# Batch 0's scatter places cast one by one on GpSimd, and block plans cut to the blocks they have

## The chip, the cores and the metric

The kernel runs on one core of one Trainium2 chip. The metric is device microseconds of one execution. The kernel before was timed three times: 1270.5, 1272.84 and 1274.08 us, median 1272.84 us.

A core has a matrix engine (TensorE, PE in the profile; PEld is its loading of stationary operands), a vector engine (VectorE, DVE), a scalar engine (ScalarE, ACT), GpSimd (POOL) and SyncE (SP), which here only issues DMAs. Each engine works through its own instructions in order and waits on semaphores for the others.

## The reference

Two blocks follow each other: an FNet mixing (the real part of a two-dimensional Fourier transform over sequence and feature) and a mixture of experts without dropped tokens, in which each token goes to the one expert with the largest logit.

```python
x: (8, 2496, 256)                                  # batch, sequence, feature
X = np.fft.fft(np.fft.fft(x, axis=1), axis=2).real
x = X.reshape(8 * 2496, 256)                       # 19968 tokens
logits = x @ w_gate                                # w_gate (256, 8)
expert_idx = np.argmax(logits, axis=1)
probs = softmax(logits)                            # 1e-9 added to the sum
for e in range(8):                                 # tokens sorted by expert
    h = np.maximum(x_sorted[lo:hi] @ w1[e], 0.0)   # w1 (8, 256, 1024)
    y_sorted[lo:hi] = h @ w2[e]                    # w2 (8, 1024, 256)
return gate_w[:, None] * y                         # in the tokens' own order
```

## The kernel before

The eight batches of the input go through four stages, and later batches' early stages are woven into earlier batches' late ones.

1. `first(b)`: SP loads the batch in three thirds (tile `xq`, line 289), VectorE folds it (`fold`, lines 295 to 306: wide additions and subtractions of two operands), TensorE makes the first Fourier step, and the result goes to DRAM (`Td`, line 342) and back in another layout (`regroup`, line 354).
2. `second(b)`: the further Fourier steps, in two halves of ten tiles of 128 rows. For each tile ScalarE and VectorE write the transformed rows to the tile `rows` (lines 384 and 410) and the logits to `lg` (408).
3. `route(b, h, rows, lg)`: once per half. VectorE finds each token's expert; TensorE counts ranks (`rk`); VectorE sums up the place of each token in the sorted buffer `Xs` in DRAM (lines 450 to 455). The places come out as a 128 x 10 tile, one column for each of the ten tiles, and the ten scatters are put on the list `waiting`.
4. `send()` takes one scatter from that list: an indirect DMA on GpSimd's queue (`put_row`, line 236), which writes 128 rows of 258 floats to the places in an int32 column `pi`. For batches 1 to 7 the place is float: ScalarE copies the column to a small tile `due` (line 468) and GpSimd casts it to `pi` (line 469). For batch 0 VectorE writes the int32 tile `pi` in the last addition of the places (line 453), and the scatter follows without a cast.

When both halves of a batch are routed, `close(b)` runs `plan(b, size, k, last)` for each block size of that batch's round: which rows of `Xs`, of which expert, each of the `k` blocks takes. This is a string of about 20 small VectorE operations on one partition (lines 488 to 521), and it leaves a table `tab`. The round of batch 0 has a plan of 2 blocks of 256 tokens and one of 4 blocks of 128; then follow 4 of 256, 3 of 512, and 5 of 512 for each of the batches 3 to 7; the last round also has 7 of 256 and 21 of 128. `MOST` is the largest of these counts, 21, and the plan's larger tiles are all made for 21 entries.

`experts(todo)` then works through the blocks. SP reads an entry of the table into registers and loads the block's weights (`fetch_weights`, lines 544 and 546) and its rows from `Xs` (`fetch_rows`, four DMAs from line 534 and one from line 538). The read of rows waits until all scatters of the batches in that round have landed; the loading of weights only needs the table. VectorE transposes the rows (line 582), TensorE makes the two products with a ReLU between them (lines 796 and 798), and the scaled rows go out by indirect DMA from GpSimd.

The order is fixed when the program is built. Batch 0 goes first: `send()` is called once after each step of `second(0)`, so that the first half's scatters are issued while the second half is being transformed; what is left of them is issued before the first block. After that, steps of batch b + 1 are put between the blocks of batch b - 1's and b's rounds by a counter of due steps.

Of the kernel before, what the change touches and what calls it, by code (L numbers as in the profile page):

```python
# [15 lines left out]
ALU = mybir.AluOpType  # L16
ACTF = mybir.ActivationFunctionType
AX_X = mybir.AxisListType.X
# [17 lines left out]
E, F = 8, 1024  # L36
# [14 lines left out]
def bc(ap, axis, n):  # L51
    shape = list(ap.shape)
    shape.insert(axis, n)
    return ap[tuple([slice(None)] * axis + [None])].to_broadcast(shape)
# [75 lines left out]
def rounds():  # L130

    want = [((256, 2), (128, 4)), ((256, 4),)] + [((512, B),)] * (B - 2)
    plan, used = [], 0

    def full(done, size):
        return max(0, -(-(done - used - E * (size - 1)) // size))

    for b in range(B):  # L140
        done = (b + 1) * S
        now = []
        for size, most in want[b]:
            k = min(full(done, size), most)
            if k:
                now.append((size, k, False))
            used += size * k
        if b == B - 1:
            k = full(done, BLK)
            used += BLK * k  # L150
            now.append((BLK, k, False))
            now.append((REST, (NT - used + E * (REST - 1)) // REST, True))
        plan.append(now)
    return plan
# [33 lines left out]
MOST = max(k for now in rounds() for _, k, _ in now)  # L188
# [27 lines left out]
def kernel(ctx: ExitStack, tc, x, w_gate, w1, w2, out):  # L216
    nc = tc.nc
    vec, act, pool = nc.vector, nc.scalar, nc.gpsimd

    def mm(o, lhsT, rhs, start=True, stop=True, **kw):  # L220
        nc.tensor.matmul(o, lhsT=lhsT, rhs=rhs, start=start, stop=stop, **kw)  # L221
# [13 lines left out]
    def put_row(dst, idx, rows, last, group):  # L235
        return unordered(pool.indirect_dma_start(  # L236
            out=dst, out_offset=bass.IndirectOffsetOnAxis(ap=idx, axis=0),
            in_=rows, in_offset=None, bounds_check=last, oob_is_err=False), group)


    def sent(ins, b):
        tc.declare_no_dep(ins, group="taken", reason="no block before this batch's round has these rows")
        tc.add_to_no_dep_group(f"xs{b}", ins)
# [25 lines left out]
    con, k = {}, 0  # L269
# [146 lines left out]
    def route(b, h, rows, lg):  # L416

        nonlocal base

        def small(name, *dims, dt=F32):  # L420
            return sp.tile([128, *dims], dt, tag=name, name=name)

        mx, eq, v = small("mx", NSL), small("eq", NSL, E), small("v", NSL)
        vec.reduce_max(mx[:], lg[:], axis=AX_X)
        vec.tensor_tensor(eq[:], lg[:], bc(mx[:], 2, E), op=ALU.is_equal)
        vec.tensor_tensor(eq[:], eq[:], bc(con["rev"][:], 1, NSL), op=ALU.mult)
        vec.reduce_max(v[:], eq[:], axis=AX_X)
        vec.tensor_tensor(v[:], v[:], con["good"][:, h], op=ALU.mult)
        oh = small("oh", NSL + 1, E, dt=BF16)
        vec.memset(oh[:, NSL], 0.0)  # L430
        vec.tensor_tensor(oh[:, 0:NSL], bc(con["rev"][:], 1, NSL), bc(v[:], 2, E), op=ALU.is_equal)
        yield

        su = small("su", NSL)
        vec.tensor_tensor(lg[:], lg[:], bc(mx[:], 2, E), op=ALU.subtract)
        act.activation(lg[:], lg[:], ACTF.Exp)
        vec.tensor_scalar(rows[:, :, D], con["row"][:, h], float(b * S), None, op0=ALU.add)
        yield

        rk = pm_.tile([128, NSL + 1, E], F32, tag="m", name="rk")  # L440
        mm(rk[:], tri[:], oh[:], True, False)
        for s in range(NSL):
            mm(rk[:, s + 1:], ones[:], bc(oh[:, s], 1, NSL - s), False, s == NSL - 1)
        vec.reduce_sum(su[:], lg[:], axis=AX_X)
        vec.tensor_scalar(su[:], su[:], 1e-9, None, op0=ALU.add)
        vec.reciprocal(rows[:, :, D + 1], su[:])
        yield

        pos, pf, pi = small("pos", NSL, E), small("pf", NSL), small("pi", NSL, dt=I32)
        vec.tensor_tensor(pos[:], rk[:, 0:NSL], bc(base[:], 1, NSL), op=ALU.add)  # L450
        vec.tensor_tensor(pos[:], pos[:], oh[:, 0:NSL], op=ALU.mult)
        vec.reduce_sum(pf[:], pos[:], axis=AX_X)
        vec.tensor_tensor(pf[:] if b else pi[:], pf[:], con["far"][:, h], op=ALU.add)
        nxt = cp.tile([128, E], F32, tag="base", name="base", bufs=2)
        vec.tensor_tensor(nxt[:], rk[:, NSL], base[:], op=ALU.add)
        base = nxt
        for s in range(NSL):
            waiting.append((b, pf[:, s:s + 1], pi[:, s:s + 1], rows[:, s]))
# [3 lines left out]
    def send():  # L462

        if waiting:
            b, place, idx, rows = waiting.popleft()
            if b:
                due = sp.tile([128, 1], F32, tag="due", name="due", bufs=8)
                act.copy(due[:], place)  # L468
                pool.tensor_copy(idx, due[:])  # L469
            sent(put_row(Xs, idx, rows, E * CAP - 1, "xs"), b)  # L470


# [2 lines left out]
    bk = {n: bt[:, lo:hi] for n, (lo, hi) in where.items()}  # L475
    gone = bk["cap"]

    def plan(b, size, k, last):

        nonlocal gone  # L480

        def one(name, *dims, dt=F32):
            return cp.tile([1, *dims], dt, tag="p_" + name, name="p_" + name, bufs=2)

        nb, ni = one("nb", E), one("ni", E, dt=I32)
        ce, ex, rb, n = one("ce", E), one("ex", E), one("rb", E), one("n", E)
        lo = one("lo", E, E)
        vec.tensor_tensor(nb[:], base[0:1], gone[:], op=ALU.subtract)
        vec.tensor_scalar(ni[:], nb[:], size - 1.0 if last else 0.0, None, op0=ALU.add)
        vec.tensor_scalar(ni[:], ni[:], size.bit_length() - 1, None, op0=ALU.logical_shift_right)  # L490
        vec.tensor_copy(nb[:], ni[:])
        vec.tensor_tensor(lo[:], bk["low"].rearrange("p (a b) -> p a b", a=E), bc(nb[:], 1, E), op=ALU.mult)
        vec.reduce_sum(ce[:], lo[:], axis=AX_X)
        vec.tensor_tensor(ex[:], ce[:], nb[:], op=ALU.subtract)
        yield
        vec.scalar_tensor_tensor(rb[:], ex[:], -float(size), gone[:], op0=ALU.mult, op1=ALU.add)
        ge, ei = one("ge", MOST, E), one("ei", MOST)
        val, eq, rw = one("val", MOST, E + 1), one("eq", MOST, E + 1), one("rw", MOST)
        vec.tensor_tensor(ge[:], bc(bk["i"], 2, E), bc(ce[:], 1, MOST), op=ALU.is_ge)
        vec.reduce_sum(ei[:], ge[:], axis=AX_X)  # L500
        yield
        vec.tensor_tensor(eq[:], bc(ei[:], 2, E + 1), bc(bk["e9"], 1, MOST), op=ALU.is_equal)
        vec.memset(val[:, :, E:E + 1], float(E * CAP))
        vec.scalar_tensor_tensor(val[:, :, 0:E], bc(bk["i"], 2, E), float(size), bc(rb[:], 1, MOST),
                                 op0=ALU.mult, op1=ALU.add)
        yield
        vec.tensor_tensor(val[:], val[:], eq[:], op=ALU.mult)
        vec.reduce_sum(rw[:], val[:], axis=AX_X)
        tab = cp.tile([1, 2, MOST], I32, tag="p_tab", name="p_tab", bufs=4)
        vec.tensor_copy(tab[:, 0], rw[:])  # L510
        vec.tensor_scalar(tab[:, 1], ei[:], E - 1.0, None, op0=ALU.min)
        if last:
            cnt = cp.tile([1, 1], I32, name="cnt")
            vec.tensor_copy(cnt[:], ce[:, E - 1:E])
            tabs["cnt"] = cnt
        if not last:

            vec.tensor_scalar(n[:], ex[:], -1.0, float(k), op0=ALU.mult, op1=ALU.add)
            vec.scalar_tensor_tensor(n[:], n[:], 0.0, nb[:], op0=ALU.max, op1=ALU.min)
            nxt = one("gone", E)  # L520
            vec.scalar_tensor_tensor(nxt[:], n[:], float(size), gone[:], op0=ALU.mult, op1=ALU.add)
            gone = nxt
        yield
        tabs[b, size, last] = tab
# [340 lines left out]
    def close(b):  # L865

        for size, k, last in rounds()[b]:
            yield from plan(b, size, k, last)
# [68 lines left out]
    for k, _ in enumerate(second(0)):  # L937
        if k % 2 == 0:
            next(early, None)
        send()  # L940
    work = experts(todo)
    steps = {b: mixed(b) for b in range(1, B)}
    for b in range(1, B):

        done, due, room = 0, 0.0, 0.0
# [81 lines left out]
```

## Time and profile before

| | |
|---|---|
| median of three timed runs | 1272.84 us |
| the profiled execution's own time | 1280.92 us |
| its span, first to last instruction | 1279.1 us |
| mean granted clock of TensorE | 0.972 |
| PE busy | 1221.0 us, 95% |
| DVE busy | 700.4 us, 55% |
| ACT busy | 436.3 us, 34% |
| POOL busy | 398.3 us, 31% |
| scatters to `Xs` (line 236) | 160, mean 1020 ns |
| casts on GpSimd (line 469) | 140, mean 282 ns |

All durations come from one profiled execution, which took 8.08 us longer than the median of the timed runs. The page's rows of 40 slices give the busy share of an engine in tenths, a slice being 32 us. "PEclk" is the clock that the throttle granted TensorE, in tenths of full speed. In a group or timeline row, "out<-in" names the tiles written and read, and what stands behind "idle before" is the engine that ended the wait, as far as semaphores show it; "issue" is time for which no wait is seen. A line number is that of the kernel's text; several callers can share a helper's line, such as 236 for all indirect DMAs and 221 for all matmuls.

### The profile page before, as it was taken

Reading aid. Unit: us, or ns where it says so; the run is one execution under the profiler, and the core shown is the slowest. Engines: PE = TensorE matmul, PEld = TensorE weight load, DVE = VectorE, ACT = ScalarE, POOL = GpSimd, SP = SyncE. Lnnn points to the kernel's source line nnn. Section 1 sums busy time; section 2 is a strip of 40 time slices with the busy share of each in tenths; the row PEclk is TensorE's granted clock in tenths of the full one; section 3 lists DMA queues with packets and bytes.
Section 4 is the critical chain, followed back from the end, with each engine's and each line's share of the span. In section 5 each row is a group of like instructions: output and inputs, shape, how many; then the busy total and the mean of one; then the engine's idle time right before and its main releaser. Section 6 shows DMA issues by size and latency. Waiting matters only on the chain.

```text
span 1279.1 us, 21208 instructions
## 1 busy us (share of the span) xinstructions
PE 1221.0 (95%) x6905; PEld 1077.0 (84%) x6905; DVE 700.4 (55%) x1772; ACT 436.3 (34%) x1096; POOL 398.3 (31%) x495
## 2 busy tenths in 40 slices
PE   6768999999999999999999999999999999999996
PEld 4557898876788888888888888888889999999995
DVE  4455434343466655564556455674578774444662
ACT  1423332332243433434343343432333332222232
POOL 0235327145116311561116411461453321111112
PEclk6859999999999999999999999999999999999998
DMA  8859798765348553573336434443435238778786
GB/s 241 279 181 321 242 339 297 204 228 175 125 146 260 162 153 113 175 240 114 104 118 211 144 120 149 132 152 107 130 121 167 91 129 296 283 277 276 280 279 246
DMA packets 163211, 249.72 MB, mean 195 GB/s; under 512 B 118601, under 2 KB 130227, under 8 KB 143516
## 3 DMA queue, kind: packets, MB, share of 16 engines
q1 hardware_dynamic: 146327, 203.28, 50.0%
q0 software_dynamic: 15888, 42.14, 9.1%
q10 hardware_dynamic: 885, 2.94, 0.7%
q8 instruction: 56, 0.92, 0.3%
q14 instruction: 55, 0.45, 0.1%
HBM read 194.91 MB, written 54.83 MB: 195 GB/s over the span
## 4 chain that ended last, share of the span: by engine, by line
PE 87%; DMA 6%; DVE 3%; another core or an unknown queue 2%; issue 1%; ACT 1%; SPq 0%; POOL 0%; POOLq 0%; DVEq 0%; ACTq 0%
PE py L221 32%; PE ph L221 10%; PE c L221 10%; PE a L221 10%; PE p L221 6%; PE d L221 6%; PE b L221 5%; PE e L221 4%; PE s L221 3%; DMA xq<-in_x_dram 2%; DMA Td<-t 1%; DMA t<-Td 1%; DMA xb<-Xs 1%; PE rk L221 0%
## 5 line engine op out<-in xcount | busy, mean ns | idle before, releaser
L221 PE MATMUL py<-w_sb,hT 128*128 128x256 f32 x2016 | 454.9, 380 | 1.3 <-DVE hT L796 1.3
L221 PEld LDWEIGHTS py<-w_sb,hT 128*128 128x128 f32 x2016 | 377.6, 190 | 51.2 <-DVE hT L796 1.7
L236 POOL DMA_INDIRECT out_dram<-y,ro x163 | 160.4, 984 | 694.0 <-ACT y L837 482.6
L236 POOL DMA_INDIRECT Xs<-rows,pi x160 | 163.2, 1020 | 109.9 <-DVE rows L410 52.1
L221 PE MATMUL ph<-xT,w_sb 128*128 128x128 f32 (+2 forms) x992 | 171.3, 328 | 6.1 <-DVE hT L796 3.3
L221 PEld LDWEIGHTS ph<-xT,w_sb 128*128 128x128 f32 x992 | 135.5, 192 | 30.5 <-issue 17.9
L837 ACT ACTIVATE y<-py,xb 128x256 f32<-128x256 f32 x129 | 61.0, 473 | 239.5 <-PE py L221 213.0
L221 PE MATMUL a<-xT,w_sb 128*128 128x256 f32 (+1 forms) x512 | 117.5, 356 | 0.0
L621 DVE TENSOR_TENSOR u<-p,b 128x512 f32<-128x512 f32 x57 | 39.1, 687 | 124.2 <-PE b L221 95.0
L796 DVE TENSOR_SCALAR hT<-ph 128x512 f32<-128x512 f32 x43 | 29.7, 690 | 129.5 <-issue 79.2
L221 PEld LDWEIGHTS a<-xT,w_sb 128*128 128x128 f32 x512 | 89.5, 190 | 10.7 <-DVE xT L582 0.4
L408 DVE COPY lg<-p 128x16 f32<-128x16 f32 x80 | 13.9, 174 | 141.5 <-ACT zs L405 121.3
L631 ACT ACTIVATE hT<-a 128x512 f32<-128x512 f32 x57 | 34.0, 597 | 149.5 <-PE a L221 115.7
L585 ACT ACTIVATE xT<-xT 128x256 f32<-128x256 f32 (+1 forms) x94 | 36.4, 387 | 121.8 <-DVE xT L582 71.9
L221 PE MATMUL s<-xq,w 104*112 104x256 f32 (+2 forms) x208 | 62.6, 426 | 11.0 <-DVE xq L297 10.9
L221 PEld LDWEIGHTS p<-table,t 120*128 120x128 f32 x352 | 55.2, 206 | 15.0 <-ACT zz L379 5.5
L221 PE MATMUL p<-table,zz 128*128 128x145 f32 (+1 forms) x320 | 57.2, 304 | 7.6 <-ACT t L321 5.5
L221 PE MATMUL p<-table,t 120*128 120x120 f32 (+1 forms) x352 | 57.7, 291 | 6.1 <-ACT zz L379 4.1
L221 PE MATMUL c<-xT,ws 128*128 128x256 f32 (+1 forms) x256 | 59.5, 359 | 3.2 <-DVE hT L627 3.2
L469 POOL CAST pi<-due 128x1 int32<-128x1 f32 x140 | 39.5, 282 | 69.1 <-ACT due L468 68.7
L582 DVE STREAM_TRANSPOSE xT<-xb 128x512 f32<-128x512 f32 (+1 forms) x94 | 58.2, 625 | 4.3 <-DMA xb<-Xs 4.3
L798 ACT ACTIVATE hT<-ph 128x512 f32<-128x512 f32 x55 | 32.8, 597 | 80.2 <-PE ph L221 64.9
(146 smaller groups left out, 1798.1 us busy)
## 6 DMA issues: line engine op xcount, KB each, us to landing
w_sb<-in_moe_w_dram SPq DMA_DIRECT2D x132, 1024.0 KB
xq<-in_x_dram SPq DMA_DIRECT2D x24, 896.0 KB
xb<-Xs SPq DMA_DIRECT2D x112, 128.0 KB
Td<-t SPq DMA_DIRECT2D x18, 448.0 KB
t<-Td SPq DMA_DIRECT2D x8, 768.0 KB
t<-Td SPq DMA_DIRECT2D x8, 640.0 KB
xb<-Xs SPq DMA_DIRECT2D x52, 64.0 KB
xb<-Xs SPq DMA_DIRECT2D x100, 32.0 KB
```

The costliest lines, as they stand in the source:

```text
L221: nc.tensor.matmul(o, lhsT=lhsT, rhs=rhs, start=start, stop=stop, **kw)
L236: return unordered(pool.indirect_dma_start(out=dst, out_offset=bass.IndirectOffsetOnAxis(ap=idx, axis=0), in_=rows, in_offset=None, bounds ...
L408: vec.tensor_copy(lg[:, k:k + 2], p3[:, NY:NY + 2 * E].rearrange("p (m e) -> p m e", m=2))
L469: pool.tensor_copy(idx, due[:])
L582: vec.transpose(free(xT[:], 256 * h, [32, n // 32], [BIG, 2], [1, 32]), free(xb, 512 * h, [64, n // 32], [1, 2], [2, 32]))
L585: act.activation(odd, odd, ACTF.Copy, scale=-1.0)
L621: vec.tensor_tensor(u2[:], p1[:], b[:], op=add)
L631: act.activation(h11, a[:], ACTF.Relu)
L796: vec.tensor_scalar(o, ph[:], 0.0, None, op0=ALU.max)
L798: act.activation(o, ph[:], ACTF.Relu)
L837: act.activation(y[:], py[:], ACTF.Copy, scale=meta[:, i, 1:2])
```

## The change

It has two parts. In `route`, the last addition of the places writes the float tile `pf` for batch 0 as for the others, and in `send` GpSimd casts each column to `pi` ahead of its scatter; for batch 0 directly from `pf`, without the copy on ScalarE. In `plan`, the tiles `ge`, `val`, `eq`, `ei` and `rw` are used up to `k` entries instead of `MOST`, and so is the table.

```diff
@@ route
-        vec.tensor_tensor(pf[:] if b else pi[:], pf[:], con["far"][:, h], op=ALU.add)
+        vec.tensor_tensor(pf[:], pf[:], con["far"][:, h], op=ALU.add)
@@ send
             if b:
                 due = sp.tile([128, 1], F32, tag="due", name="due", bufs=8)
                 act.copy(due[:], place)
-                pool.tensor_copy(idx, due[:])
+                place = due[:]
+            pool.tensor_copy(idx, place)
             sent(put_row(Xs, idx, rows, E * CAP - 1, "xs"), b)
@@ plan
-        ge, ei = one("ge", MOST, E), one("ei", MOST)
-        val, eq, rw = one("val", MOST, E + 1), one("eq", MOST, E + 1), one("rw", MOST)
-        vec.tensor_tensor(ge[:], bc(bk["i"], 2, E), bc(ce[:], 1, MOST), op=ALU.is_ge)
-        vec.reduce_sum(ei[:], ge[:], axis=AX_X)
+        ge, val, eq = (one(name, MOST, E + 1)[:, 0:k] for name in ("ge", "val", "eq"))
+        ei, rw = (one(name, MOST)[:, 0:k] for name in ("ei", "rw"))
+        count = bk["i"][:, 0:k]
+        vec.tensor_tensor(ge[:, :, 0:E], bc(count, 2, E), bc(ce[:], 1, k), op=ALU.is_ge)
+        vec.reduce_sum(ei, ge[:, :, 0:E], axis=AX_X)
         yield
-        vec.tensor_tensor(eq[:], bc(ei[:], 2, E + 1), bc(bk["e9"], 1, MOST), op=ALU.is_equal)
+        vec.tensor_tensor(eq, bc(ei, 2, E + 1), bc(bk["e9"], 1, k), op=ALU.is_equal)
         vec.memset(val[:, :, E:E + 1], float(E * CAP))
-        vec.scalar_tensor_tensor(val[:, :, 0:E], bc(bk["i"], 2, E), float(size), bc(rb[:], 1, MOST),
+        vec.scalar_tensor_tensor(val[:, :, 0:E], bc(count, 2, E), float(size), bc(rb[:], 1, k),
                                  op0=ALU.mult, op1=ALU.add)
         yield
-        vec.tensor_tensor(val[:], val[:], eq[:], op=ALU.mult)
-        vec.reduce_sum(rw[:], val[:], axis=AX_X)
+        vec.tensor_tensor(val, val, eq, op=ALU.mult)
+        vec.reduce_sum(rw, val, axis=AX_X)
         tab = cp.tile([1, 2, MOST], I32, tag="p_tab", name="p_tab", bufs=4)
-        vec.tensor_copy(tab[:, 0], rw[:])
-        vec.tensor_scalar(tab[:, 1], ei[:], E - 1.0, None, op0=ALU.min)
+        vec.tensor_copy(tab[:, 0, 0:k], rw)
+        vec.tensor_scalar(tab[:, 1, 0:k], ei, E - 1.0, None, op0=ALU.min)
```

## The prediction, made before the changed kernel was run

> **What bounds the kernel now.** I read the page first, its busy times and slices, then the stretches of the start, then the queue waits and timelines of the stage that the change touches.
>
> ```profile
> PE 1221.0 (95%) x6905; PEld 1077.0 (84%) x6905; DVE 700.4 (55%) x1772; ACT 436.3 (34%) x1096; POOL 398.3 (31%) x495
> PE   6768999999999999999999999999999999999996
> PEclk6859999999999999999999999999999999999998
> ...
> 240.00:1240.00 1000.00, 996.67 (x5647) 885.20 (x5646) 574.81 (x1334) 351.83 (x842) 305.76 (x370) 1.00 0.54 175
> ```
>
> Columns of the last row: stretch, its length, busy time of PE, PEld, DVE, ACT, POOL (GpSimd), granted clock, DMA share, GB/s. From 240 to 1240 us TensorE idles 3.3 us; there nothing else bounds. The loss is in the first four slices: batch 0 must be transformed, routed and scattered to DRAM before the first expert block can be read back. A change there shifts everything behind it; one later is worth only what it takes from those 3.3 us.
>
> How batch 0's 20 scatters leave GpSimd (timeline of POOL: start, duration, instruction, idle before it):
>
> ```profile
> 52.53 1.11 POOL L236 DMA_INDIRECT Xs<-rows,pi  x1 [52.08 <-DVE rows L410]
> 53.94 0.97 POOL L236 DMA_INDIRECT Xs<-rows,pi  x1 [0.30 <-issue]
> ...
> 64.16 0.97 POOL L236 DMA_INDIRECT Xs<-rows,pi  x1 [0.30 <-issue]
> 65.44 1.77 POOL L236 DMA_INDIRECT Xs<-rows,pi  x1 [0.31 <-issue]
> 67.51 1.57 POOL L236 DMA_INDIRECT Xs<-rows,pi  x1 [0.30 <-issue]
> ...
> 78.33 0.97 POOL L236 DMA_INDIRECT Xs<-rows,pi  x1 [0.31 <-issue]
> ```
>
> They are issued back to back for 27 us: GpSimd's own pitch sets the last one. The second half's places were ready at 63.6, before the first half was through (65.1), so nothing else holds the row up. Who waits for them (waits of the DMA queues; then the timeline of SP and DVE):
>
> ```profile
> SPq L534 <- DMA Xs<-rows,pi: 7.7, 2, 4.8
> ...
> 83.46 1.92 SPq L534 DMA_DIRECT2D xb<-Xs  x4
> ...
> 89.25 0.70 DVE L582 STREAM_TRANSPOSE xT<-xb 128x512 f32<-128x512 f32 x1
> ...
> 90.01 1.45 PE L221 MATMUL ph<-xT,w_sb 128*128 128x256 f32 x4 [1.75 <-DVE ro L755]
> ```
>
> SP's read of the first block waits for the landing of all 20 (the last landing event is at 83.21), then transpose, then the first expert matmul at 90.01, with TensorE idle 1.75 us before it. Behind L534 on SP's queue stand the weights of the next block (90.45), batch 1's store and batch 2's input load (91.45, 91.92): they all move with it.
>
> **The change, part by part.**
>
> *1. Twenty casts on GpSimd.* Batch 0's places stay float, and each scatter gets its own cast in front. The instruction order of all other engines is unchanged. How cast and scatter follow each other is shown by batch 1, which does this already:
>
> ```profile
> 123.26 0.98 POOL L236 DMA_INDIRECT Xs<-rows,pi  x1 [0.28 <-issue]
> 124.23 0.20 POOL L469 CAST pi<-due 128x1 int32<-128x1 f32 x1
> 124.71 0.98 POOL L236 DMA_INDIRECT Xs<-rows,pi  x1 [0.28 <-POOL pi L469]
> ...
> 132.94 0.80 POOL L469 CAST pi<-due 128x1 int32<-128x1 f32 x1
> ```
>
> Pitch before: (64.16 - 53.94) / 8 = 1.278 us. With casts: 124.71 - 123.26 = 1.45 us. The cast's 0.20 us plus 0.28 us to its scatter replaces an issue gap of 0.30 us, so a cast costs 0.17 us, not the 0.28 of its row's mean. The first one is free: 0.93 us lay between the places (51.60) and the first scatter; in batch 1 it is 0.89 us from the ready value (102.67) over cast to scatter (103.56). Sum: 19 x 0.17 = +3.3 us at the last issue.
>
> *2. Holds by VectorE.* The scatters at 65.44 and 67.51 took 0.8 and 0.6 us more than the rest, and ended 0.85 to 0.95 us after a wide two-input VectorE operation of the fold (65.15 to 66.36; 66.95 to 68.15) that had begun before them; the cast at 132.94 took 0.80 and likewise ended with such an operation. Between 65 and 83 us VectorE has four such stretches (also 72.06 and 80.38, about 1.2 us each); the scatters met two. Twice as many GpSimd starts, and a row that now reaches past 80.4, will meet the other two. Bounds: 0 (they slip by again) to 2 x 1.2 = 2.4; I take the middle, since a start falls anywhere within one: +1.2. GpSimd ends its row 4.5 us later.
>
> The Trainium skill, "SBUF — State Buffer", section "Who interferes with whom", says that a VectorE instruction with two SBUF inputs and a GpSimd one that reads SBUF exclude each other for the whole instruction, the second waiting; the rows above agree. By that rule a cast, which reads SBUF, is exposed each time and the upper bound would hold: POOL +5.7 us. The rule speaks against this change.
>
> *3. From last issue to first matmul.* Two covers exist in the profiled execution. The last scatter landed 3.9 us after its issue ended (79.30 to 83.21), because 2 MB of weights (71.2 to about 80) ran beside it; the first scatter's landing events begin 1.6 us after its issue. So up to 2.3 us are absorbed. And the block's last landing (87.61) precedes its transpose (89.25) by 1.64 us, as VectorE first waits for TensorE's work on batch 1. Together 3.9 us. But that lateness of TensorE hangs on waits that no queue of the program explains (chain of waits: start, length):
>
> ```profile
> 61.21 2.81 another core or an unknown queue
> ...
> 64.22 4.78 another core or an unknown queue
> ...
> 75.20 3.89 another core or an unknown queue
> 79.21 2.06 another core or an unknown queue
> ```
>
> They sum to 13.5 us, and the profiled execution took 1280.92 us (span 1279.1) where the median of the three timed runs is 1272.84, 8.1 less. If part of them belongs to being profiled, TensorE and the weights are earlier in a timed run, and both covers are gone, while GpSimd's row stays. Bounds of the absorption: 0 to 3.9 us; I take 0 for the timed runs, as the 8.1 us exceed the covers. The shift is then the full +4.5 us.
>
> *4. Other waits of part 1.* Behind the casts GpSimd has only the scatters, and idles 23.4 us after them. Batch 1's place sums on VectorE (101.6, 118.0) newly wait for the casts of the same buffer, done by about 67 and 84: nothing. Batch 1's first routed rows (79.85) wait for the first ten scatters, which end 2 to 3 us later but 10 us before: nothing; with that cover gone, at most those 3 us, inside the shift already counted.
>
> *5. Shorter plans.* Six VectorE operations per plan work on 8 or 9 entries per block instead of per 21 (groups by shape, first 140 us; mean ns behind the busy time):
>
> ```profile
> L507 DVE TENSOR_TENSOR p_val<-p_val,p_eq 1x189 f32<-1x189 f32 x3 | 1.0, 342 | 0.0
> L492 DVE TENSOR_TENSOR p_lo<-bt,p_nb 1x64 f32<-1x64 f32 x3 | 0.6, 213 | 0.2 <-DVE p_nb L491 0.2
> L488 DVE TENSOR_TENSOR p_nb<-base,p_gone 1x8 f32<-1x8 f32 x2 | 0.3, 154 | 0.1
> ```
>
> 8 elements take 0.15 us, 64 take 0.21, 189 take 0.34: 1 ns per element on 0.15. The six take 1.94 us now. A plan of 2 blocks (16 to 18 elements) saves 0.95 us, of 3 0.90, of 4 0.86, of 5 0.80, of 7 0.68, that of 21 nothing. The eleven plans (2, 4, 4, 3, five of 5, 7, 21) save 0.95 + 2 x 0.86 + 0.90 + 5 x 0.80 + 0.68 = 8.2 us of VectorE's 700. Nearly all lies beside TensorE. On the path: batch 0's first plan releases weights at 71.2, needed only at 90: nothing. Batch 1's plan (118.6 to 123.2) stands before the ReLU that TensorE waits 3.3 us for, but 2.43 us of idle follow it before that ReLU (125.62). Bounds 0 to -0.86; I take half, -0.4. In the 1000 us after 240 at most 3.3 us can be won; as single waits there are a few tenths, I take 0.
>
> Sum: +3.3 + 1.2 - 0 - 0.4 = **+4.1 us**. The profiled execution would be 1285.0; on the median, 1272.84 + 4.1 = **1276.9**.
>
> **The rivals.** A difference under 0.3% (3.8 us) is about what a measurement of this kernel can't tell from none.
>
> - *Hidden anyway*: both covers hold in timed runs. +4.5 - 3.9 - 0.8 = -0.2: **1272.6**, not slower. For it: the landing and the transpose as profiled. Against: the 8.1 us. It decides from a cover of about 1 us on.
> - *The clock falls too*: the granted clock was 0.5 from 59.99 to 87.30 and again from 90.71 to 94.12, after a stretch of 3.41 us in which TensorE was busy only 1.66. A longer wait at 88 adds one or two such stretches, each 3.41 / 2 = 1.7 us of matmuls: +4.1 + 3.4 = 7.5, **1280.3**. Against: between 116 and 136 TensorE waits for others, which can swallow it.
> - *VectorE counted more than it seems*: the casts cost nothing, and the shorter plans take all 3.3 us of idle after 240, 0.86 at 123 and 0.8 of earlier weights: -5.0, **1267.8**. Against: no wait on a plan's tile is among the long ones. It decides where the casts cost under 1.2 us.
>
> On the second rival the Trainium skill, "TensorE: Matmul & The Clock Gate", section "What's actually happening", says that an idle window of about 3.4 us halves the clock and a busy one restores it. The rows agree on the length, but here a half-busy stretch sufficed.
>
> **How the numbers follow.** Forecast 0.50, hidden 0.22, clock 0.17, VectorE 0.11. The forecast's own bounds: 3.3 + 0 - 3.9 - 0.9 at the very least, 3.3 + 2.4 at the most (1278.5). Its 1276.9 lies just past 1276.66, so 0.29 of its 0.50 is slower. Slower: 0.29 + 0.16 (clock) + 0.02 = 0.47; same: 0.21 + 0.19 (hidden) + 0.03 = 0.43; faster: 0.10. The range takes in hidden with its scatter (1271) and the clock case with 1.2 more (1281.5); VectorE's case stays out.
>
> **What would show it.** Part 1: POOL pitch 1.45 us from 52.5, last issue ending 82.6 to 85. Part 2: casts or scatters over 0.5 and 1.2 us beside the folds. Part 3: SP's first L534 at 85 to 88, first block matmul 2 to 4.5 us later. Part 5: the six plan operations at 0.16 to 0.19 us. Wrong if the first block matmul stays at 90, if the clock row falls for longer, or if batch 1's stage to 140 us reorders its DMA traffic.

## The result

The changed kernel is slower by 0.2%: 1275.37 us against 1272.55 us, medians of 21 runs each on the same chip, ratio 1.0021 [1.0011, 1.0031]. That is 2.7 us more (1.4 to 3.9). 1276.9 us had been forecast, from a sum of +4.1 us; the sum lies just above the interval.

In this section and the next ones, "us more" is a ratio less 1, times the median of the kernel before on the same chip. A ratio is not exactly the quotient of the two medians. The series ran on several chips, on which the kernel before has medians from 1272.55 to 1285.32 us. A ratio compares runs on one chip, but profiles of different series are in general not from the same chip, and a difference of a few us between them may be the chip's.

The first page lines of the kernel after: busy times, TensorE's share and granted clock in 40 slices of 32 us.

```profile
PE 1221.4 (96%) x6905; PEld 1079.7 (85%) x6905; DVE 693.8 (54%) x1772; ACT 437.4 (34%) x1096; POOL 406.2 (32%) x515
PE   5759999999999999999999999999999999999996
PEclk9959999999999999999999999999999999999998
```

TensorE does the same work and is still partly idle in the first three slices. VectorE loses 6.6 us of busy time (700.4 before), GpSimd gains 7.9 (398.3 before): the two parts of the change are both there. The span is 1273.4 us, shorter than the 1279.1 of before, though the timed runs are longer: the profile of before was 8 us over its own median, that of after sits on it (its own time is 1275.13). So the two spans can't be compared, and the stages must be.

GpSimd's row of batch 0 (timeline of POOL, kernel after):

```profile
52.66 0.18 POOL L470 CAST pi<-pf 128x1 int32<-128x1 f32 x1 [52.21 <-DVE pf L453]
53.61 1.13 POOL L236 DMA_INDIRECT Xs<-rows,pi  x1 [0.78 <-ACT zz L379]
...
62.66 0.99 POOL L236 DMA_INDIRECT Xs<-rows,pi  x1 [0.28 <-POOL pi L470]
63.65 0.76 POOL L470 CAST pi<-pf 128x1 int32<-128x1 f32 x1
64.69 2.10 POOL L236 DMA_INDIRECT Xs<-rows,pi  x1 [0.28 <-POOL pi L470]
...
68.79 0.98 POOL L236 DMA_INDIRECT Xs<-rows,pi  x1 [0.28 <-ACT t L321]
69.76 0.41 POOL L470 CAST pi<-pf 128x1 int32<-128x1 f32 x1
...
73.35 0.98 POOL L236 DMA_INDIRECT Xs<-rows,pi  x1 [0.28 <-POOL pi L470]
74.32 0.20 POOL L470 CAST pi<-pf 128x1 int32<-128x1 f32 x1
74.80 0.98 POOL L236 DMA_INDIRECT Xs<-rows,pi  x1 [0.28 <-POOL pi L470]
...
76.25 1.51 POOL L236 DMA_INDIRECT Xs<-rows,pi  x1 [0.28 <-POOL pi L470]
...
84.04 0.98 POOL L236 DMA_INDIRECT Xs<-rows,pi  x1 [0.28 <-POOL pi L470]
```

Undisturbed, scatter follows scatter after 74.80 - 73.35 = 1.45 us, where it was 1.278 before. From the first start to the last it is 30.43 us (84.04 - 53.61), and was 25.80: 4.6 us more. Four instructions took clearly longer than their kind: 0.56, 1.12, 0.21 and 0.53 us more. The timeline of VectorE in the same stretch has the folds beside them:

```profile
63.16 1.21 DVE L306 TENSOR_TENSOR xq<-xq 104x1024 f32<-104x1024 f32 x1
64.65 0.67 DVE L295 TENSOR_TENSOR xq<-xq 104x508 f32<-104x508 f32 x1
65.24 0.67 DVE L296 TENSOR_TENSOR xq<-xq 104x508 f32<-104x508 f32 x1
...
68.91 1.21 DVE L306 TENSOR_TENSOR xq<-xq 104x1024 f32<-104x1024 f32 x1
...
76.23 0.68 DVE L295 TENSOR_TENSOR xq<-xq 104x508 f32<-104x508 f32 x1
76.82 0.68 DVE L296 TENSOR_TENSOR xq<-xq 104x508 f32<-104x508 f32 x1
```

Each of the four ended within 0.9 us after a stretch of folds (64.41 after 64.37, 66.79 after 65.91, 70.17 after 70.12, 77.76 after 77.50). All four stretches held one instruction; before, two did. The two scatters that had begun ahead of a fold and ran on beside it, at 62.66 and 68.79, kept their length (0.99 and 0.98 us), and so did the folds (1.21 us).

What follows the row: the waits of the DMA queues from 60 to 140 us (in total, how many, the longest), then SP's first read of rows, the transpose and the first expert matmul in the timelines of SP, DVE and PE.

```profile
SPq L536 <- DMA Xs<-rows,pi: 16.7, 2, 8.4
```

```profile
86.75 1.92 SPq L536 DMA_DIRECT2D xb<-Xs  x4
```

```profile
90.40 0.71 DVE L584 STREAM_TRANSPOSE xT<-xb 128x512 f32<-128x512 f32 x1 [7.30 <-DMA xb<-Xs]
```

```profile
91.17 3.78 PE L221 MATMUL ph<-xT,w_sb 128*128 128x256 f32 x8 [9.15 <-DVE ro L757]
```

Now TensorE waits 9.15 us for this block, not 1.75, and VectorE waits 7.30 us for its rows, where the transpose waited for nothing before. SP's wait for the scatters grew from 7.7 to 16.7 us. The chain of waits (kernel after) runs straight through GpSimd's row:

```profile
82.59 0.98 POOL Xs L236
83.56 0.21 POOL pi L470
83.77 0.27 issue
84.04 2.47 DMA Xs<-rows,pi
86.75 0.35 SPq L536
...
88.36 1.92 DMA xb<-Xs
90.40 0.71 DVE xT L584
91.17 3.77 PE ph L221 x8
...
123.19 0.15 DVE p_gone L523
123.34 0.61 DVE hT L798
```

The pieces "another core or an unknown queue" are not in this chain up to 260 us. In the chain before they made 13.5 us ahead of the first block, and 7.6 us more behind it, of which the first piece stood between batch 1's plan and the ReLU:

```profile
123.19 2.41 another core or an unknown queue
125.62 0.69 DVE hT L796
```

So the idle time behind that plan, for which the prediction halved the plan's term, was itself such a wait. The last two lines of the chain after show the plan directly ahead of the ReLU, with no idle between: there it is on the path.

The groups by shape in the first 140 us (mean ns behind the busy time) show the shorter plan operations, and the stretches view the steady part:

```profile
L509 DVE TENSOR_TENSOR p_val<-p_val,p_eq 1x36 f32<-1x36 f32 x2 | 0.5, 266 | 0.0
```

```profile
240.00:1240.00 1000.00, 999.30 (x5690) 889.29 (x5689) 576.75 (x1340) 354.06 (x846) 308.27 (x370) 1.00 0.54 177
```

Over all eleven plans the six operations took 13.2 us, 21.7 before. After 240 us TensorE idles 0.7 us, 3.3 before.

### The profile page after: what moved, and what is told of

Same layout as the page of the kernel before. It is cut to its first block, busy times and chain, and to the rows that moved or that the text cites. A ratio compares the mean times of both kernels' runs of the same rounds, so it can differ in the third digit from the quotient of the medians.

```text
span 1273.4 us, 21239 instructions
## 1 busy us (share of the span) xinstructions
PE 1221.4 (96%) x6905; PEld 1079.7 (85%) x6905; DVE 693.8 (54%) x1772; ACT 437.4 (34%) x1096; POOL 406.2 (32%) x515
## 4 chain that ended last, share of the span: by engine, by line
PE 88%; DMA 6%; DVE 3%; issue 1%; SPq 1%; ACT 1%; POOL 0%; POOLq 0%; DVEq 0%; ACTq 0%
PE py L221 33%; PE ph L221 10%; PE c L221 10%; PE a L221 10%; PE p L221 6%; PE d L221 6%; PE b L221 5%; PE s L221 4%; PE e L221 4%; DMA xq<-in_x_dram 2%; DMA t<-Td 1%; DMA w_sb<-in_moe_w_dram 1%; DMA Xs<-rows,pi 1%; SPq L536 0%; PE rk L221 0%
## 5 line engine op out<-in xcount | busy, mean ns | idle before, releaser
L221 PE MATMUL d<-xT,w_sb 128*128 128x256 f32 (+1 forms) x256 | 58.7, 356 | 0.0
```

## The experiments

The question was which part carries the 2.7 us, whether GpSimd's row passes into the time in full (the forecast) or is covered (the first rival), and what the plans return. Every ratio is to the kernel before on the same chip.

### One part at a time

**Casts alone**: the kernel before with the changes in `route` and `send`; the plans stay at 21 entries.

```diff
-        vec.tensor_tensor(pf[:] if b else pi[:], pf[:], con["far"][:, h], op=ALU.add)
+        vec.tensor_tensor(pf[:], pf[:], con["far"][:, h], op=ALU.add)
...
-                pool.tensor_copy(idx, due[:])
+                place = due[:]
+            pool.tensor_copy(idx, place)
```

> The casts alone, with the plans as before. Theory PATH (GpSimd's row of scatters sets when the first expert block can be read, and nothing covers it): 19 casts by 0.17 us plus about 1.2 us of holds, +3.3 to +4.5 us against before, pitch of the scatters 1.45 us. Rival COVER (part of the longer row is absorbed by the landing and by the slack ahead of the transpose): +0 to +2 us at the same pitch. Rival VECTORE (the shorter plans pay back a lot): the casts alone cost +5 us or more.

Measured: 1282.93 against 1278.46, ratio 1.0029 [1.0015, 1.0044], 3.7 us more (1.9 to 5.6). The row took 30.74 us from first to last start. The first block, in the timelines of DVE and PE:

```profile
90.29 0.71 DVE L583 STREAM_TRANSPOSE xT<-xb 128x512 f32<-128x512 f32 x1 [10.69 <-DMA xb<-Xs]
```

```profile
91.06 3.78 PE L221 MATMUL ph<-xT,w_sb 128*128 128x256 f32 x8 [12.54 <-DVE ro L756]
```

So the casts cost, and VectorE and TensorE both stand still for over 10 us until the rows are there: in this profile neither of the two covers is left.

**Plans alone**: the changed kernel with `route` and `send` as before.

```diff
-        vec.tensor_tensor(pf[:], pf[:], con["far"][:, h], op=ALU.add)
+        vec.tensor_tensor(pf[:] if b else pi[:], pf[:], con["far"][:, h], op=ALU.add)
...
-                place = due[:]
-            pool.tensor_copy(idx, place)
+                pool.tensor_copy(idx, due[:])
```

> The shorter plans alone, batch 0's places written as int32 by VectorE as before. PATH: only batch 1's plan is on the path, -0.4 us (between 0 and -0.9). COVER: 0, since the measured +2.7 us of both is then the casts alone. VECTORE: -2 to -5 us.

Measured: 1279.98, ratio 0.9999 [0.9981, 1.0017], 0.1 us less (2.4 less to 2.2 more). It was run once more, in the last series:

> The kernel of e2 once more, since e10 came out 2 us above what e2 and e4 add up to. If shorter plans gain what e6 and e8 give per us of VectorE time (batch 1: 0.86 of 3.9 us of lengthening, about -0.6 us; later ones about -0.3) and nothing at batch 0, where the scatters end later: -0.9 us, an interval of e2 and e12 together around 0 to -1. If earlier weights cost something, as e10 would have it: +1 to +3 us, with the first half's scatters landing later than in before (the first rows of batch 1 wait for them).

Measured there: 1270.55 against 1274.21, ratio 0.9973 [0.9956, 0.9990], 3.4 us less (1.3 to 5.6). The intervals of the two series meet only between -2.4 and -1.3 us; weighted together they give about 1.9 us less. By the second series the plans alone made the fastest kernel seen here; the first can't tell it from the kernel before. The first block of the second series, in the timeline of PE:

```profile
85.05 3.78 PE L221 MATMUL ph<-xT,w_sb 128*128 128x256 f32 x8 [9.07 <-DVE ro L756]
```

That is 5 us earlier than in the profile of before, which is from another series, with a row of the old length (25.33 us); why is taken up below.

### Is it the casts' time on GpSimd?

**Two casts**: casts alone, with a second cast of the same place, to a tile that nobody reads, ahead of each of batch 0's.

```diff
+            if not b:
+                spare = sp.tile([128, 1], I32, tag="spare", name="spare", bufs=8)
+                pool.tensor_copy(spare[:], place)
             pool.tensor_copy(idx, place)
```

> As e1, with a second, unused cast ahead of each of batch 0's 20 scatters. PATH: the second cast stands directly behind another one, so it costs its whole duration, 20 by 0.20 us: +4 us more than e1, about +8 us against before, pitch 1.65 us. COVER: what was absorbed in e1 is used up, so the step from e1 to e3 is larger than the step from before to e1. VECTORE says nothing of the step.

Measured: 1286.3, ratio 1.0052 [1.0030, 1.0075], 6.6 us more (3.8 to 9.6). Timeline of POOL:

```profile
60.34 0.98 POOL L236 DMA_INDIRECT Xs<-rows,pi  x1 [0.28 <-ACT rows L384]
61.33 0.23 POOL L472 CAST spare<-pf 128x1 int32<-128x1 f32 x1
61.50 0.17 POOL L473 CAST pi<-pf 128x1 int32<-128x1 f32 x1
61.95 0.98 POOL L236 DMA_INDIRECT Xs<-rows,pi  x1 [0.28 <-POOL pi L473]
```

The pitch is 1.61 us: a second cast costs another 0.16, not the 0.20 that had been expected. The row takes 33.88 us, and the time grows with it.

**One wide cast** per half instead of ten narrow ones, ahead of the half's first scatter; the plans stay at 21 entries.

```diff
-            waiting.append((b, pf[:, s:s + 1], pi[:, s:s + 1], rows[:, s]))
+            waiting.append((b, pf[:, s:s + 1], pi[:, s:s + 1], rows[:, s], () if s else (pi[:], pf[:])))
...
+            if b:
+                pool.tensor_copy(idx, place)
+            elif whole_half:
+                pool.tensor_copy(*whole_half)
```

> Batch 0's places are cast on GpSimd, but ten columns at once, one cast per half. PATH: the first cast lies where GpSimd waits anyway, the second costs 0.2 to 0.5 us: +0.2 to +0.5 us against before. If the cost came from handing the places from VectorE to GpSimd and not from twenty more instructions in the row: as e1.

Measured: 1280.18, ratio 1.0002 [0.9988, 1.0017], 0.3 us more (1.5 less to 2.2 more). Ten columns are cast in the time of one, and the scatters keep their old pitch (timeline of POOL):

```profile
53.03 0.20 POOL L473 CAST pi<-pf 128x10 int32<-128x10 f32 x1 [52.58 <-DVE pf L453]
53.99 1.13 POOL L236 DMA_INDIRECT Xs<-rows,pi  x1 [0.76 <-ACT zz L379]
55.42 0.97 POOL L236 DMA_INDIRECT Xs<-rows,pi  x1 [0.30 <-issue]
```

The same conversion on the same engine, without the growth of the row, costs nothing that can be measured. What costs is that the casts stand one by one between the scatters. In the length of the row against the 26.3 us that the two profiles of the kernel before average (25.80 and 26.78), the three kernels read:

| kernel | row, us | more than 26.3 | time, us more |
|---|---|---|---|
| one wide cast | 27.19 | 0.9 | 0.3 (-1.5 to 2.2) |
| casts alone | 30.74 | 4.4 | 3.7 (1.9 to 5.6) |
| two casts | 33.88 | 7.6 | 6.6 (3.8 to 9.6) |

The other nine rows without single casts, in the profiles of all series, run from 25.33 to 27.34 us, so the 0.9 of the wide cast is within their spread. For the other two it is some 0.85 us of time for each us of row: in this series, with the plans at 21 entries, the row passes nearly in full. What a longer stretch of TensorE at half clock costs (see the rivals below) is in these times too.

**A wide cast that nothing waits for**: the kernel before, with GpSimd casting each half's places to a tile that nobody reads.

```diff
+            elif half is not False:
+                spare = sp.tile([128, NSL], I32, tag="spare", name="spare")
+                pool.tensor_copy(spare[:], half[:])
             sent(put_row(Xs, idx, rows, E * CAP - 1, "xs"), b)
```

> Before, with one unused cast on GpSimd ahead of each half's ten scatters of batch 0; the places are still written as int32 by VectorE and no scatter waits for the cast. All six profiles without such a cast have waits of several us between 60 and 82 us that nothing in the program ends, the four with one have none. If a GpSimd instruction that takes VectorE's signal itself is what removes them, they are gone here too; if the scatters' own wait on the cast does it, or if it is chance, they are there. On the time: the row of scatters grows by under 1 us, so +0 to +1 us if those waits are covered in timed runs; -2 us or more if timed runs of before pay for them.

Measured: 1278.92 against 1280.12, ratio 0.9994 [0.9977, 1.0011], 0.8 us less (2.9 less to 1.4 more): no effect that shows.

### Where the plans count

Here the six wide operations of some plans, in the kernel before, are done three times (the repeats write the same values again). For the plans of batch 1:

```diff
+        times = 3 if b == 1 else 1
+        for _ in range(times):
+            vec.tensor_tensor(ge[:], bc(bk["i"], 2, E), bc(ce[:], 1, MOST), op=ALU.is_ge)
+            vec.reduce_sum(ei[:], ge[:], axis=AX_X)
```

> Before, with the six wide operations of batch 1's plan done three times each (the result is the same): 2 x 1.94 = 3.9 us more on VectorE at about 120 us. Theory ON PATH (the ReLU that TensorE waits for stands behind that plan): +2 to +3.9 us. Rival BESIDE: within 1 us.

Measured: 1286.98 against 1285.32, ratio 1.0020 [1.0004, 1.0035], 2.6 us more (0.5 to 4.5) for 3.9 us of work.

For batch 0's two plans (`3 if b == 0`), 7.8 us of work:

> Before, with the same done to the two plans of batch 0: 7.8 us more on VectorE between 66 and 82 us, weights of the first block 3.9 us later. ON PATH: +4 to +7.8 us. BESIDE (the wait for the scatters covers it, 7 to 10 us of idle on VectorE ahead of the first transpose): within 1 us, at most +2.

Measured: 1288.52, ratio 1.0036 [1.0021, 1.0051], 4.6 us more (2.7 to 6.6). The first block's matmul in the timeline of PE is late because VectorE is, and the rows had long been there:

```profile
97.14 3.36 PE L221 MATMUL ph<-xT,w_sb 128*128 128x256 f32 x7 [1.76 <-DVE ro L759]
```

For all later plans (`3 if b > 1`), 31 us of work:

> Before, with the same done to the eight plans of batches 2 to 7: 31 us more on VectorE after 240 us. ON PATH (a plan holds up TensorE's operands): +5 us or more, which would make shorter plans worth a few us there. BESIDE: within 2 us.

Measured: 1286.89, ratio 1.0012 [0.9998, 1.0026], 1.5 us more (0.3 less to 3.3 more). Of 31 us almost all lies beside TensorE; the longest wait of TensorE after 240 us is among the last plans (timeline of PE):

```profile
856.76 1.57 PE L221 MATMUL c<-xT,ws 128*128 128x256 f32 x4 [2.03 <-DVE hT L631]
```

So the plans of batches 0 and 1 lie on the path or close to it, the rest beside it. That was shown by making them longer; what they return when they are made shorter need not be the same.

### Were the waits without a releaser the profiler's?

The forecast took the 13.5 us of such waits in the profile of before for a part of being profiled. The kernel before, unchanged, was profiled once more:

> The kernel before, unchanged, for a second profile. If the waits without a releaser belong to one profiled execution and not to the kernel, they are gone here, the transpose of the first block waits for its rows, the first block matmul starts at 87 to 88.5 us (as in e4, whose row of scatters is the same but for two casts) instead of 90.0, and TensorE idles 8 us or more before it. If they belong to the kernel, it starts at 90 again.

Measured: 1277.71 us in its profiled run, against a median of 1285.32, so 7.6 us shorter, not longer. But the waits were there again (timeline of ACT, waits marked "remote"; then that of PE):

```profile
63.75 0.17 ACT L372 COPY t<-pr 120x6 f32<-120x6 f32 x1 [5.00 <-remote]
68.05 0.36 ACT L379 COPY zz<-p 128x240 f32<-128x240 f32 x1 [4.13 <-remote]
```

```profile
88.26 2.01 PE L221 MATMUL ph<-xT,w_sb 128*128 128x256 f32 x8 [1.76 <-DVE ro L755]
```

A profiled run can be 7 us faster than the median and have them, so they need not belong to a long run. It is a single run, shorter than all 29 timed runs behind that median; what made the first profiled run of before long stays open.

The next thought was that they belong to kernels whose scatters follow each other without a cast, since the profiles with single casts lacked them between 60 and 82 us. Against it stood a version of the change with one wide cast per half and the short plans:

> The changed kernel with one cast of ten columns per half in place of twenty single ones: the change's second part at the smallest price of the first. PATH: +0.3 for the casts and -0.4 to -2 for the plans, so -0.1 to -1.7 us against before, and 3 to 4 us under the changed kernel in the same call.

Measured: 1280.84 against 1280.12, ratio 1.0019 [1.0004, 1.0033], 2.4 us more (0.5 to 4.2). That is outside what was expected: neither the wide cast nor the short plans had cost anything alone. In its profile the first block is late again with the rows already there, as in both profiles of before (timeline of PE):

```profile
89.90 2.01 PE L221 MATMUL ph<-xT,w_sb 128*128 128x256 f32 x8 [1.76 <-DVE ro L760]
```

It has long waits of this kind too, the longest in its chain of waits being

```profile
122.18 8.03 another core or an unknown queue
```

The changed kernel was run beside it once more:

> The changed kernel unchanged, to stand beside e10 on one chip: +2.7 us against before as measured at first (interval +1.4 to +3.9); first block matmul at 91 us again in the profile.

Measured: 1281.92, ratio 1.0023 [1.0010, 1.0035], 2.9 us more (1.3 to 4.5), as in the first series. That does not fit the price of the row found above. The two kernels of this series differ by 0.5 us in their ratios and 1.1 in their medians, where 3 to 4 had been expected, though their rows took 26.42 and 30.23 us. The profiles agree with the small difference, 89.90 against 90.56 us for the first block: with the shorter row, the block waited for TensorE's and VectorE's late work on batch 1 instead. Against it, the plans alone and the whole change, measured in different series, differ by 2.8 to 6.3 us for the same casts. So that the casts cost time is shown; that with the short plans a row shorter by 4 us returns nearly as much is not.

The chain of waits of this second profile of the changed kernel has one piece without a releaser, at a later place:

```profile
125.14 7.26 another core or an unknown queue
```

By TensorE's next count of ranks (180.38 us, 174.02 in the profile shown above) it has lost 7 us, though its first block was 0.6 us earlier, and its span is 1280.3 us, 6.9 more. So here the wait goes with lost time. But the timed medians of the two series differ as much (1281.92 and 1275.37 us), each profile lying close to its own; whether executions differ here or chips, the record does not tell. Of the kernels without a cast, the plans alone had one at 77.88 us in the first series and none in the second.

For whom the engines waited can be read from the semaphore events of the traces. Over all fourteen profiles, all but one of these waits of ScalarE and VectorE end at a signal on one semaphore, which 984 of TensorE's instructions raise and no DMA does. (The exception, 1.83 us at 79.70 with batch 0's plans long, ends at a signal of VectorE's own.) The views name no releaser because the signal came more than 1.5 us, up to 8.3, after the end that the trace gives the last matmul that raises it; for the other waits on this semaphore the median is 0.014 us. So they are waits for TensorE, not for another core or queue. Whether its matmuls ran longer than the trace has them or it signalled late, and why, stays open. In the first profile of the changed kernel and the second of the plans alone, no signal that ended a wait came more than 0.02 us after that end. Between 60 and 85 us such waits stand in nine of the ten profiles without single casts and in none of the four with them; whether the casts have a part in that is open, too.

## Why the prediction was right, and where its steps were not

**Part 1** (+3.3) held: pitch 1.45 us, and the first cast nearly free. From its ready value (52.59) over the cast to the first scatter it is 1.02 us, and was 0.93.

**Part 2** (+1.2) held in mechanism and size. The holds that can be told in the two rows are 2.4 us after (0.56 + 1.12 + 0.21 + 0.53) and 1.4 before (0.8 + 0.6), so +1.0; the bounds had been 0 and 2.4. The Trainium skill, "SBUF — State Buffer", section "Who interferes with whom", by which the second of the two instructions waits for the first one's end, agrees with the four ends above, each after the fold's. It does not show in the two scatters that had begun first: neither they nor the folds beside them were longer. The higher price that the prediction drew from it (+5.7 for the row, a whole 1.2 us in each of two more stretches) did not come: all four stretches met an instruction, but each held it for 0.2 to 1.1 us only. The row grew by 4.6 us between the two profiles, 4.5 predicted.

**Part 3** took the covers as 0. For the time this was nearly right: 4.4 us of row gave 3.7. The reason given for it fell, so that this term came out near is in part luck. The waits without a releaser are waits for TensorE; the second profile of before has them in a run below its median, so the 8.1 us were no measure of them, and that timed runs are free of them is not shown. Nor did the expected sign in the profile come: the first block's matmul is 1.2 us later than before (91.17 against 90.01), not 2 to 4.5, since the profile of before has its covers. Against the second profile of before (88.26) it is 2.9 later.

The first of the covers goes with the time at which the weights are loaded. In twelve profiles SP's second load of the first weights, the end of the last scatter's issue, and SP's first read of rows read:

| kernel | second weights issued | row ends | first read, after row's end |
|---|---|---|---|
| batch 0's plans long | 81.12 | 78.95 | 3.6 |
| before | 72.62 | 79.30 | 4.2 |
| batch 1's plan long | 75.82 | 83.09 | 3.5 |
| before, again | 72.34 | 79.98 | 3.3 |
| later plans long | 73.83 | 82.02 | 2.7 |
| unused cast | 73.30 | 82.00 | 1.8 |
| plans alone | 71.98 | 81.17 | 1.7 |
| one wide cast | 72.00 | 82.15 | 1.7 |
| plans alone, again | 67.12 | 78.63 | 2.0 |
| wide cast, short plans | 71.53 | 83.23 | 1.7 |
| casts alone | 69.24 | 84.88 | 1.6 |
| after | 68.40 | 85.02 | 1.7 |

The first line is of another kind: there SP issued the weights only after the row, and its read stood behind them without a wait for the scatters. In the others, where the row ends 8.7 us or more after that load, SP reads within 2 us (1.6 us in the two profiles left out, two casts and after, again); where it ends sooner, the read is late by up to 2.5 us more. That agrees with the prediction's reading that the weights beside it made the last landing slow, but no run moved the weights alone. By this reading a longer row runs out of that shadow, and so a part of it can be hidden. How large that part is in a timed run can't be read from a profile; the casts alone bound it: 4.4 us of row less 3.7 us of time is 0.7, and by the interval of that run 0 to 2.5.

**Part 4** (nothing) held in the sum, not in its detail. Batch 1's first rows did come to wait for batch 0's first scatters, for 6.8 us where at most 3 had been allowed for, in the chain of the kernel after:

```profile
68.79 6.82 DMA Xs<-rows,pi
75.70 0.62 DVE rows L410 x2
```

At 67.85 and 68.40 us the first weights were issued, 3 to 4 us sooner than before, into the landing of the first half. GpSimd's row went on back to back meanwhile, and TensorE later waited 9.15 us for the block that this row sets, which covers it.

**Part 5** (-0.4) is the term that was mis-sized, if one was. The whole change cost 2.7 us (2.9 when run again) and the casts alone 3.7, so the plans return about 1, with intervals that also allow nothing or 3; the two series of the plans alone say 0.1 and 3.4, not agreeing well, and with the wide cast the short plans returned nothing. The time that they take off VectorE was predicted well (8.5 us, 8.2 predicted). The step of it that is in doubt is "batch 0's first plan releases weights at 71.2, needed only at 90: nothing". The long plans of batch 0 cost 4.6 us, though that came by VectorE's time, and if the table above is read rightly, weights that start sooner clear the way for the last scatters: in the second series of the plans alone they were issued at 67.12, and its first block began 5 us before that of the kernel before. How much of that is the plans' doing, how much the absence of waits without a releaser from that profile, and how much the other chip's, stays open. For batch 1's plan, 2.6 us of time for 3.9 of work is 0.67 per us; by that, the 0.86 us that it loses would be worth 0.6 (an estimate), where 0.4 was taken, halved for an idle time that was a wait for TensorE.

After 240 us nothing was predicted, at most 3.3. TensorE's idle time there, by the profiles, with plans of 21 entries: 3.3 and 2.1 us (before, twice), 2.4 (casts alone), 3.9 (two casts), 2.8 (one wide cast), 2.1 (unused cast), 3.9 and 3.9 (batch 1's and batch 0's plans long), in the mean 3.1; with the later plans long it is 6.3. With short plans: 0.7 and 1.9 (after, twice), 2.2 and 1.7 (plans alone, twice), 1.7 (wide cast), in the mean 1.6. So it may be that the short plans win about 1.5 us there. But the waits of before lie late, the longest at 958 us (timeline of PE, kernel before), 1.18 us where the prediction had only a few tenths, and its last plan had ended at 866:

```profile
958.32 1.13 PE L221 MATMUL c<-xT,ws 128*128 128x256 f32 x4 [1.18 <-DVE hT L627]
```

So if these 1.5 us are the plans' doing, it is not by an operation that stands in the way there. This was not tested.

**The rivals.** *Hidden anyway* is out as a full cover: the changed kernel and the casts alone are slower beyond their intervals, and with long plans the time grows with the row. A cover in part is not out, as the pair with short plans shows. *The clock falls too* had its condition: between 55 and 140 us the granted clock was at half for 34.1 us (58.4 to 68.6 and 72.0 to 95.9), and for 30.7 before (60.0 to 87.3 and 90.7 to 94.1); this sign, named in the prediction as one of being wrong, came. In the other profiles with single casts it is 34.1 to 37.5 us, in the second profile of before 27.3. The first block's eight matmuls took 3.78 us, 3.16 before, and 1.89 at full clock. The rival's full price did not come, since the time is not near +7.5; what part of the 2.7 us it makes was not separated. The mean clock of the whole profile can't tell it: 0.981 against 0.972, since in that of before the clock was also at half from 8.8 to 39.5 us. *VectorE counted more*: its condition, casts that cost under 1.2 us, did not hold with long plans; the plans may well return more than 0.4, but not 5.

So the time came out near the forecast by a sum in which +3.3 and +1.2 are shown for the row. That the row passes into the time is shown with the plans at 21 entries, while with the short plans the one comparison within a series speaks against it. Covers of 0 were nearly right for a reason that was wrong, and a gain of the plans somewhat larger than 0.4 fits the rest without being settled.

## What to carry to other kernels

On an engine that issues indirect DMAs back to back, a small operation between two of them lengthens the row by its addition to the pitch (0.17 us here), and where the last of them releases the next stage and nothing else is as late, that is paid in time. Convert all the indices of a group at once: ten columns took the 0.20 us of one, though with the short plans this did not make the kernel measurably faster than single casts did. Before a cover is counted or dropped, look at several executions: here both profiles of the kernel before had covers ahead of the first block, and that of nearly the same kernel with the casts alone had none.

## What had not been expected of the hardware

In some profiled executions TensorE's signals come 1.5 to 8.3 us after the ends that the trace gives its matmuls, and the engines that wait for them stand still with no releaser named: none up to 260 us in one profile of the changed kernel, one of 7.3 us at 125 us in the other, which had lost 7 us by 180 us. Neither the profiler nor the absence of a cast explains them by itself. And the landing of an indirect scatter goes with what was started up to 8 us earlier: 1.6 to 2.0 us from the end of its issue to the read that waits for it where the weights' load was 8.7 us or more before, 2.7 to 4.2 us where it was nearer.
